# Gate and up matmuls, and the convolution's among them, as pairs of 64-row tiles ordered by GpSimd tokens

## The chip, the cores and the metric

The kernel runs on one core of one Trainium2 chip. A core has a matrix engine (TensorE, PE in the profile; its weight loads are PEld), a vector engine (VectorE, DVE), an activation engine (ScalarE, ACT), GpSimd (POOL) and SyncE (SP), which here issues nearly all DMAs. The engines run their own instruction queues in order and wait for one another by semaphores. The metric is the device time of one execution in microseconds (us). Engine times below are from one profiled execution.

## The reference

A block of a network with adaptive layer norm: a long gated convolution, then a gated MLP, both added to the input. Sequence length S is 2048, width D 576, hidden width F 4608, all in bfloat16.

```python
mod = (silu(c) @ w_mod).reshape(c.shape[0], 6, 1, -1)      # sa, ca, ga, sb, cb, gb
h = layernorm(x) * (1 + ca) + sa
x = x + ga * A(h, k, v, shift_k, ssm_k, ssm_D)
h = layernorm(x) * (1 + cb) + sb
x = x + gb * ((silu(h @ w1) * (h @ w3)) @ w2)

def A(q, k, v, shift_k, ssm_k, ssm_D):
    kv = causal_conv(k, shift_k, taps=4) * v
    y = irfft(rfft(pad(kv)) * rfft(pad(ssm_k)))[:S] + kv * ssm_D
    return q * y
```

## The kernel before

**The convolution.** The sequence is cut into 8 blocks of 256 rows. Each block is transformed with small cosine and sine bases held in `Fb` and `Fk` (functions `forward`, `forward2`: matmuls of 288 columns from L299 and L313, followed by a ScalarE copy). The spectra `X` and `V` are multiplied and summed on VectorE (`pair`, L405 to L412), and `inverse` (L539) transforms the sums back. `k_rows` (L364) turns the filter's rows with TensorE transposes into one PSUM tile, which ScalarE copies out. `turn` (L571) does the same with the normed rows, and `turned` (L601) writes them, scaled and shifted, into `h2T`, the MLP's input. Layer norm statistics come from ScalarE sums (`junk`, L440), and six small GpSimd instructions make the scales of them (`ln_scales`, L455 to L460).

**The MLP.** The 2048 rows are handled in four row blocks of 512. For each, `stream` makes the hidden rows `h3`, and `down` multiplies them by `w2` (L974). The 4608 hidden columns are 36 pieces of 128; an item of `stream` is one such piece for 512 rows (or two pieces for 256 rows). An item needs gate and up, each a sum over D = 576 = 4 x 128 + 64. `full` does the four full 128-row matmuls of gate and of up (L911). `rest` does the last 64 rows (L922): w1's last 64 rows lie in partitions 0 to 63 and w3's in 64 to 127 of the same weight slot, so the two run side by side in the two halves of the array. Then `hide` lets ScalarE apply silu to the gate (`sg`, L929), copy the up half (`u`, L931), and VectorE multiply them (`h`, L933).

Items are taken in groups of `size`: two everywhere, four in the last row block, where no convolution is left. For the first half of a group `full` comes first and `rest` after; for the second half `rest` comes first and `full` later, so the 64-row matmuls of a group stand together:

```python
for m in early:
    begin(m); full(m, True)
for m in early: rest(m, False)
for m in late:
    begin(m); rest(m, True)
for m in early: hide(m)
for m in late:
    full(m, False); hide(m)
```

**Mixing the two.** The convolution of the next blocks is written as generators that yield their estimated cost. After each item `advance` runs such steps until as much cost is spent as is due. So TensorE, ScalarE and VectorE each find convolution work between the items. The first stream works on 256 rows while block 1 is convolved (33 to 72 us). The second finishes the first row block (72 to 133 us): it goes back over the first 24 pieces for rows 256 to 511 and does the remaining 12 for all 512 rows, so that groups of weights for 256 and for 512 rows alternate. The next two streams (172 to 250 us, 292 to 370 us) and the last one (408 to 480 us) are whole. A scheduler of the language sets the final order of each engine's queue from the program's order and its own estimates.

**Buffers and queues.** Weights of four pieces (w1, w3 and their last rows) fill one of two `wst` buffers, loaded by four DMAs of SyncE's queue: two of 512 KB (L866) and two of 64 KB (L867). `w2` pieces use four `w2t` buffers (L967) on the same queue, as do the loads and stores of old spectra (`Xd`, `Vd`, L417 to L433) and of the inputs. PSUM is four tiles (`ps`) of two banks each, taken in turn by all matmul results: an item holds one tile, gate in one bank and up in the other; a convolution step holds one as well. `sg` and `u` have two buffers each.

## Time and profile before

The median of three runs is 519.97 us (519.77 to 522.16). The profiled execution spans 519.5 us from its first to its last instruction; the profile gives no other time of it.

| stage | from, us | to, us | length | TensorE busy | VectorE busy | ScalarE busy |
|---|---|---|---|---|---|---|
| first block | 0 | 33.0 | 33.0 | 25.4 | 28.3 | 21.1 |
| stream, 256 rows, with block 1 | 33.0 | 72.2 | 39.2 | 35.9 | 34.2 | 25.5 |
| rest of stream 0 | 72.2 | 133.1 | 60.9 | 56.0 | 57.3 | 47.4 |
| down 0 | 133.1 | 172.2 | 39.1 | 38.7 | 30.3 | 15.9 |
| stream 1 | 172.2 | 250.5 | 78.3 | 78.3 | 55.0 | 57.7 |
| down 1 | 250.5 | 292.1 | 41.6 | 39.5 | 40.9 | 16.6 |
| stream 2 | 292.1 | 370.4 | 78.3 | 78.3 | 58.8 | 53.7 |
| down 2 | 370.4 | 408.4 | 38.0 | 37.5 | 14.5 | 17.4 |
| stream 3 | 408.4 | 480.3 | 71.9 | 71.9 | 16.5 | 36.7 |
| down 3 and output | 480.3 | 519.5 | 39.2 | 35.4 | 5.5 | 1.1 |

Busy times are sums of the recorded instructions, with the ends of matmuls modelled, so that a full TensorE is not one at its peak. In the lines of the profile L911 is a line of the kernel; `ps<-h2T,wst` tells what is written from what; the number after x counts instructions; "idle before" is the engine's idle time just before such instructions, with what ended it. A line of the stages gives from:to, its length, busy time and count of PE, PEld, DVE, ACT and POOL, the granted TensorE clock, the DMA engines' share and GB/s. A line of the chain gives start, length and what ran.

### The profile page before, as it was taken

The numbers are of one execution on the slowest core, as the hardware profiler recorded it, in microseconds if no ns is written. First come the engines' busy times: TensorE is split into PE (matmuls) and PEld (weight loads), VectorE is DVE, ScalarE is ACT, GpSimd is POOL, SyncE is SP. The second block draws the span as 40 slices with busy tenths as digits, with TensorE's granted clock in tenths as the row PEclk, the third lists the DMA queues.
The fourth block names the chain that finished last, engine by engine and source line by source line (L and its number), as shares of the span: only waits on it lengthen the run. The fifth ranks groups of instructions, "written<-read, shape, count | busy, mean of one in ns | idle before, by whom it ended". The sixth has DMA issues, their size and how long they took to land.

```text
span 519.5 us, 8708 instructions
## 1 busy us (share of the span) xinstructions
PE 496.9 (96%) x3351; PEld 292.4 (56%) x3351; DVE 341.2 (66%) x515; ACT 293.0 (56%) x581; POOL 53.4 (10%) x109
## 2 busy tenths in 40 slices
PE   7889988998999999999998999999999999999997
PEld 3656765455787544444676643444578544444775
DVE  8887997999995355797999995389661212222012
ACT  6748669668553369759562465876815346445000
POOL 3403011203021001202002000120101000000000
PEclk9979999999999999999999999999999999999999
DMA  8948839757769953648999886454555553550462
GB/s 280 336 126 276 251 108 322 275 170 227 231 193 325 358 183 105 194 150 293 354 357 336 329 252 185 147 196 140 162 139 151 150 173 107 171 162 18 117 179 70
DMA packets 102205, 107.77 MB, mean 207 GB/s; under 512 B 5075, under 2 KB 94228, under 8 KB 102164
## 3 DMA queue, kind: packets, MB, share of 16 engines
q1 hardware_dynamic: 102142, 107.21, 65.5%
q8 instruction: 26, 0.43, 0.3%
q14 instruction: 15, 0.12, 0.1%
q10 hardware_dynamic: 22, 0.01, 0.0%
HBM read 96.00 MB, written 11.21 MB: 206 GB/s over the span
## 4 chain that ended last, share of the span: by engine, by line
PE 80%; DMA 10%; ACT 4%; DVE 3%; issue 1%; POOL 1%; SPq 1%; POOLq 0%; DVEq 0%; ACTq 0%
PE ps L911 44%; PE ps L974 23%; PE ps L922 7%; DMA wst<-in_B_w_dram 5%; DMA w2t<-in_B_w_dram 3%; PE ps L313 2%; PE ps L539 2%; DMA Xd<-X 1%; DMA knat<-in_A_ssm_k_dram 1%; PE ps L364 1%; PE ps L299 1%; ACT junk L440 1%; ACT sg L929 1%; PE ps L571 1%; ACT h2T L601 0%
## 5 line engine op out<-in xcount | busy, mean ns | idle before, releaser
L911 PE MATMUL ps<-h2T,wst 128*128 128x512 bf16 (+1 forms) x1344 | 268.0, 351 | 7.3 <-DMA wst<-in_B_w_dram 4.2
L911 PEld LDWEIGHTS <-wst 128*128 128x128 bf16 x1344 | 128.1, 98 | 130.3 <-issue 20.9
L929 ACT ACTIVATE sg<-ps 128x512 bf16<-128x512 f32 x144 | 86.9, 604 | 116.9 <-PE ps L922 74.2
L974 PE MATMUL ps<-w2t,h 128*128 128x288 bf16 x1152 | 145.4, 286 | 3.0 <-DMA w2t<-in_B_w_dram 2.4
L974 PEld LDWEIGHTS <-h 128*128 128x128 bf16 x1152 | 112.4, 98 | 32.3 <-issue 3.8
L933 DVE TENSOR_TENSOR h<-sg,u 128x512 bf16<-128x512 bf16 x144 | 60.3, 421 | 96.4 <-ACT u L931 96.4
L931 ACT CAST u<-ps 128x512 bf16<-128x512 f32 x144 | 84.7, 588 | 0.4 <-DVE h L933 0.4
L410 DVE TENSOR_TENSOR p<-X,V 128x3456 bf16<-128x3456 bf16 x28 | 54.6, 1952 | 5.8 <-DMA X<-Xd 5.1
L412 DVE TENSOR_TENSOR z<-z,p 128x3456 bf16<-128x3456 bf16 x28 | 54.6, 1951 | 0.2
L992 DVE TENSOR_TENSOR og<-ps,gbrow 128x288 bf16<-128x288 f32 x32 | 13.1, 449 | 48.9 <-PE ps L974 48.9
L922 PE MATMUL ps<-h2T,wst 64*128 64x512 bf16 (+1 forms) x336 | 42.9, 352 | 0.0
L440 ACT ACTIVATE junk<-x 128x576 bf16<-128x576 bf16 x54 | 37.6, 697 | 0.5
L601 ACT ACTIVATE h2T<-ps,sbcol,cbcol 128x256 bf16<-128x256 bf16 x35 | 16.7, 569 | 26.1 <-PE ps L571 26.1
L922 PEld LDWEIGHTS <-wst 64*128 64x128 bf16 x336 | 11.3, 94 | 27.5 <-issue 24.5
L455 POOL TENSOR_SCALAR l2m<-l2s 128x2 f32<-128x2 f32 x6 | 7.8, 1294 | 154.9 <-ACT junk L440 154.9
L334 DVE TENSOR_TENSOR kvt<-kh,shk 128x1152 bf16<-128x1152 bf16 x24 | 18.0, 752 | 6.8 <-DMA kh<-in_A_k_dram 6.7
L566 ACT ACTIVATE h2row<-x,l2n,l2r 128x576 bf16<-128x576 bf16 (+1 forms) x24 | 13.8, 653 | 11.4 <-POOL l2n L460 11.4
L455 POOL TENSOR_SCALAR l1m<-l1s 128x2 f32<-128x2 f32 x7 | 4.6, 662 | 141.2 <-ACT junk L440 141.2
L335 DVE TENSOR_TENSOR kv<-kv,kvt 128x1152 bf16<-128x1152 bf16 x24 | 18.1, 754 | 0.3
L315 ACT CAST X<-ps 128x576 bf16<-128x576 f32 x24 | 15.7, 666 | 0.0
L405 DVE TENSOR_TENSOR z<-X,V 128x3456 bf16<-128x3456 bf16 x7 | 13.7, 1951 | 1.4 <-DMA X<-Xd 1.4
L740 ACT CAST y<-ps 128x576 bf16<-128x576 f32 x14 | 8.4, 653 | 9.9 <-PE ps L539 9.8
(136 smaller groups left out, 353.3 us busy)
## 6 DMA issues: line engine op xcount, KB each, us to landing
wst<-in_B_w_dram SPq DMA_DIRECT2D x80, 512.0 KB, 4.7
w2t<-in_B_w_dram SPq DMA_DIRECT2D x72, 288.0 KB, 3.2
X<-Xd SPq DMA_DIRECT2D x8, 864.0 KB, 5.8
Xd<-X SPq DMA_DIRECT2D x6, 864.0 KB, 6.6
wst<-in_B_w_dram SPq DMA_DIRECT2D x80, 64.0 KB, 2.2
kh<-in_A_k_dram SPq DMA_DIRECT2D x7, 720.0 KB, 7.2
Vd<-V SPq DMA_DIRECT2D x4, 864.0 KB, 6.0
V<-Vd SPq DMA_DIRECT2D x4, 864.0 KB, 5.1
```

Of the source, the lines that this page charges most:

```text
L334: nc.vector.tensor_mul(tmp[:], kh[:, 3 - j:5 - j, :], tap(j))
L335: nc.vector.tensor_add(kv[:], kv[:], tmp[:])
L410: nc.vector.tensor_mul(p[:], X[:], V[:])
L412: nc.vector.tensor_add(z[:], z[:], p[:])
L440: self.nc.scalar.activation(junk[:], src[:, i, :], func, accum_out=out[:, col:col + 1])
L601: nc.scalar.activation(dst, src, ACT.Identity, bias=self.sbcol[:, ct:ct + 1], scale=self.cbcol[:, ct:ct + 1])
L911: nc.tensor.matmul(gus[k][:, i, a * n:(a + 1) * n], w[:, 5 * i + ct, (fi + a) * P:(fi + a + 1) * P], hT[:, ct, t0:t1], start=(first and ct ...
L922: nc.tensor.matmul(gus[k][:, i, a * n:(a + 1) * n], w[rows, 4, (fi + a) * P:(fi + a + 1) * P], hT[rows, 4, t0:t1], start=(first and a == 0 ...
L929: nc.scalar.activation(sg[:], gus[k][:, 0, :], ACT.Silu)
L931: nc.scalar.copy(u[:], gus[k][:, 1, :])
L933: nc.vector.tensor_mul(self.h3[:, f:f + m, t0:t1], sg[:].rearrange("p (a t) -> p a t", a=m), u[:].rearrange("p (a t) -> p a t", a=m))
L974: nc.tensor.matmul(acc[t], self.h3[:, f0 + f, t * P:(t + 1) * P], w[:, f, :], start=(f0 + f == 0), stop=(f0 + f == NF - 1))
```

## The change

Every gate and up matmul over 128 rows becomes two over 64 rows. An item is done in two parts. In the first, rows 0 to 63 feed the gate's bank while rows 64 to 127 feed the up bank, in side-by-side pairs for the four full pieces of D and the last 64 rows (five pairs). In the second the halves are swapped (four pairs): rows 0 to 63 feed the up bank, rows 64 to 127 the gate's. Since both halves of the rows then write each bank, one after the other, the second part must not begin before the first is done. A token sees to that: `token` issues a GpSimd memset of one element that waits for the first part's last matmul, and the second part's first matmul on the bank waits for this memset.

Between the two parts of an item, the stream issues the second part of the item before and the first part of the item after it, with a share of the convolution's steps after each part (5/9 and 4/9 of the former amount). The groups of two or four items and the parameter `size` are gone. While a stream runs, `halves` is set, and the convolution's matmuls (`forward`, `forward2`, `inverse`) go through `two_banks`, which does the same: first part, token, a pause that ends `advance`, and then the swapped part at the next `advance`. The transposes of `k_rows` and `turn` become pairs of 64-row transposes into two banks as well; `k_rows` then needs two ScalarE copies. Outside of the streams all stays 128 rows high.

```diff
--- before.py
+++ after.py
@@ -65,6 +65,44 @@
         self.xo, self.hg, self.accs, self.l1 = {}, {}, {}, {}
         self.X, self.V, self.Wl = {}, {}, {}
         self.n_w13, self.w13, self.kept = 0, {}, {}
+        self.halves = self.pause = False
+
+    def newest(self):
+        return self.nc.cur_bb.bb.instructions[-1]
+
+    def wait_for(self, later, first):
+
+        self.tc.add_manual_dep(
+            later, first.name,
+            mybir.DependencyInfo(mybir.DependencyClass.Sync, mybir.DependencyReason.DATA),
+            reason="both halves of the rows write this bank, one after the other")
+
+    def token(self):
+
+        first = self.newest()
+        self.nc.gpsimd.memset(self.tok[:], 0.0)
+        self.wait_for(self.newest(), first)
+        return self.newest()
+
+    def two_banks(self, outs, terms):
+
+        mm = self.nc.tensor.matmul
+        if not self.halves:
+            for n, term in enumerate(terms):
+                for i in range(2):
+                    mm(outs[i], *term(i, slice(0, P)), start=(n == 0), stop=(n == len(terms) - 1))
+            return
+        for swap in range(2):
+            for n, term in enumerate(terms):
+                for rows, i in ((slice(0, 64), swap), (slice(64, P), 1 - swap)):
+                    mm(outs[i], *term(i, rows), start=(swap == 0 and n == 0),
+                       stop=(swap == 1 and n == len(terms) - 1))
+                    if swap == 1 and n == 0 and i == 1:
+                        self.wait_for(self.newest(), mark)
+            if swap == 0:
+                mark = self.token()
+                self.pause = True
+                yield 0.0
 
     def ps(self, shape=(P, 2, 512), dtype=F32):
         return self.psum.tile(list(shape), dtype, name="ps", tag="ps")
@@ -74,6 +112,7 @@
         nc, const = self.nc, self.const
         nc.scalar.preload_act_table(ACT.Silu)
         self.ident = const.tile([P, P], BF16, name="ident")
+        self.tok = const.tile([1, 1], F32, name="tok")
         self.npi = const.tile([P, 1], F32, name="npi")
         self.ppi = const.tile([P, 1], F32, name="ppi")
         self.neghalf = const.tile([P, 2], F32, name="neghalf")
@@ -293,12 +332,10 @@
         nc = self.nc
         for e in range(2):
             for cs in range(2):
+                def term(cc):
+                    return lambda h, rows: (basis[rows, cc * (e + 1), cs], rhs[rows, cc, h * H:(h + 1) * H])
                 ps = self.ps()
-                for cc in range(2):
-                    for h in range(2):
-                        nc.tensor.matmul(ps[:, h, 0:H], basis[:, cc * (e + 1), cs],
-                                         rhs[:, cc, h * H:(h + 1) * H],
-                                         start=(cc == 0), stop=(cc == 1))
+                yield from self.two_banks([ps[:, h, 0:H] for h in range(2)], [term(cc) for cc in range(2)])
                 nc.scalar.copy(dst(e, cs).rearrange("p (h d) -> p h d", h=2), ps[:, :, 0:H])
                 yield 0.4
 
...
@@ -359,11 +396,22 @@
         nat = self.knat
         kT = self.kvp.tile([P, 2, D], BF16, name="kT", tag="kT")
         pt = self.ps((P, 2, 1024), BF16)
-        for cc in range(2):
-            for ct in range(5):
-                nc.tensor.transpose(pt[:, cc, ct * P:(ct + 1) * P], nat[:, ct, cc:B:2],
-                                    self.ident[:])
-        nc.scalar.copy(kT[:], pt[:, :, 0:D])
+        if self.halves:
+            for cc in range(2):
+                for ct in range(5):
+                    for half in range(2 if ct < 4 else 1):
+                        rows, at = slice(64 * half, 64 * half + 64), 320 * cc + 64 * ct
+                        nc.tensor.transpose(pt[:, half, at:at + 64], nat[rows, ct, cc:B:2],
+                                            self.ident[rows, rows])
+            for half, n in ((0, 5), (1, 4)):
+                nc.scalar.copy(_ap(kT, 64 * half, [[D, 2], [P, n], [1, 64]]),
+                               _ap(pt, 1024 * half, [[320, 2], [64, n], [1, 64]]))
+        else:
+            for cc in range(2):
+                for ct in range(5):
+                    nc.tensor.transpose(pt[:, cc, ct * P:(ct + 1) * P], nat[:, ct, cc:B:2],
+                                        self.ident[:])
+            nc.scalar.copy(kT[:], pt[:, :, 0:D])
         if 2 < s < NBLK - 1:
             self.load_k(s + 1)
         self.kT = kT
@@ -526,19 +574,16 @@
         nc.vector.tensor_sub(z[:, 1:3, :], z[:, 1:3, :], z[:, 4:6, :])
         return 3.0
 
-    def inverse(self, s, cc):
-        nc = self.nc
+    def inverse(self, s, cc, ps):
         z = self.accs[s]
-        ps = self.ps()
+
+        def term(b, cs, row):
+            return lambda h, rows: (self.Fb[rows, b, cs], z[rows, row, h * H:(h + 1) * H])
         if s < SPLIT:
             terms = [(3 * cc + (cc if e else 0), cs, 3 * e + cs) for cs in (1, 0) for e in range(2)]
         else:
             terms = [(3 * cc, 1, cc), (3 * cc, 0, 3 - cc)]
-        for i, (b, cs, row) in enumerate(terms):
-            for h in range(2):
-                nc.tensor.matmul(ps[:, h, 0:H], self.Fb[:, b, cs], z[:, row, h * H:(h + 1) * H],
-                                 start=(i == 0), stop=(i == len(terms) - 1))
-        return ps
+        yield from self.two_banks([ps[:, h, 0:H] for h in range(2)], [term(*t) for t in terms])
 
     def residual_row(self, s, cc, ps):
         nc = self.nc
@@ -568,8 +613,14 @@
 
     def turn(self, pt, cc):
         for ct in range(5):
-            self.nc.tensor.transpose(pt[:, cc, ct * P:(ct + 1) * P],
-                                     self.h2row[:, cc, ct * P:(ct + 1) * P], self.ident[:])
+            cols = slice(ct * P, (ct + 1) * P)
+            if not self.halves:
+                self.nc.tensor.transpose(pt[:, cc, cols], self.h2row[:, cc, cols], self.ident[:])
+                continue
+            for half in range(2):
+                rows, at = slice(64 * half, 64 * half + 64), 320 * cc + 64 * ct
+                self.nc.tensor.transpose(pt[:, half, at:at + 64], self.h2row[rows, cc, cols],
+                                         self.ident[rows, rows])
 
     def turn_split(self, cc):
 
...
@@ -876,8 +935,11 @@
                 break
             self.due -= c
             self.spent += c
-
-    def stream(self, r, jobs, rate, size):
+            if self.pause:
+                self.pause = False
+                break
+
+    def stream(self, r, jobs, rate):
 
 
 
...
@@ -902,26 +964,21 @@
             ws[job[0:3]] = w
 
 
-        def full(k, first):
+        def part(k, swap):
             (fc, t0, t1, _, _), fi, m = items[k]
             w, n = ws[fc, t0, t1], t1 - t0
             for a in range(m):
-                for i in range(2):
-                    for ct in range(4):
+                cols = slice((fi + a) * P, (fi + a + 1) * P)
+                for ct in range(4 if swap else 5):
+                    for rows, i in ((slice(0, 64), swap), (slice(64, P), 1 - swap)):
                         nc.tensor.matmul(gus[k][:, i, a * n:(a + 1) * n],
-                                         w[:, 5 * i + ct, (fi + a) * P:(fi + a + 1) * P], hT[:, ct, t0:t1],
-                                         start=(first and ct == 0 and a == 0),
-                                         stop=(not first and ct == 3 and a == m - 1))
-
-        def rest(k, first):
-            (fc, t0, t1, _, _), fi, m = items[k]
-            w, n = ws[fc, t0, t1], t1 - t0
-            for a in range(m):
-                for i in range(2):
-                    rows = slice(64 * i, 64 * i + 64)
-                    nc.tensor.matmul(gus[k][:, i, a * n:(a + 1) * n],
-                                     w[rows, 4, (fi + a) * P:(fi + a + 1) * P], hT[rows, 4, t0:t1],
-                                     start=(first and a == 0), stop=(not first and a == m - 1))
+                                         w[rows, 5 * i + ct if ct < 4 else 4, cols], hT[rows, ct, t0:t1],
+                                         start=swap == 0 and ct == 0 and a == 0,
+                                         stop=swap == 1 and ct == 3 and a == m - 1)
+                        if swap == 1 and ct == 0 and a == 0 and i == 1:
+                            self.wait_for(self.newest(), marks[k])
+            if swap == 0:
+                marks[k] = self.token()
 
         def hide(k):
             (fc, t0, t1, _, _), fi, m = items[k]
@@ -933,27 +990,22 @@
             nc.vector.tensor_mul(self.h3[:, f:f + m, t0:t1], sg[:].rearrange("p (a t) -> p a t", a=m),
                                  u[:].rearrange("p (a t) -> p a t", a=m))
             del gus[k]
-            self.advance(rate * 2.05)
 
         def begin(k):
             if items[k][1] == 0:
                 load(items[k][0])
             gus[k] = self.ps()
-        for k in range(0, len(items), size):
-            early, late = range(k, k + size // 2), range(k + size // 2, k + size)
-            for m in early:
-                begin(m)
-                full(m, True)
-            for m in early:
-                rest(m, False)
-            for m in late:
-                begin(m)
-                rest(m, True)
-            for m in early:
-                hide(m)
-            for m in late:
-                full(m, False)
-                hide(m)
+        self.halves = True
+        for k in range(len(items) + 1):
+            if k < len(items):
+                begin(k)
+                part(k, 0)
+                self.advance(rate * 2.05 * 5 / 9)
+            if k > 0:
+                part(k - 1, 1)
+                hide(k - 1)
+                self.advance(rate * 2.05 * 4 / 9)
+        self.halves = False
 
     def down(self, r, rate):
         nc = self.nc
@@ -1002,7 +1054,8 @@
         self.steps, self.due, self.spent = steps, due, 0.0
 
     def end(self):
-        self.advance(1e9)
+        while self.steps is not None:
+            self.advance(1e9)
 
     def run(self):
         self.setup()
...
```

## The prediction

> **What bounds the kernel now.** I read the page first, then the stages, then the chain of work that ended last, then what sits next to it: weight loads, PSUM evacuation, GpSimd.
>
> ```profile
> span 519.5 us, 8708 instructions
> PE 496.9 (96%) x3351; PEld 292.4 (56%) x3351; DVE 341.2 (66%) x515; ACT 293.0 (56%) x581; POOL 53.4 (10%) x109
> ...
> wst<-in_B_w_dram SPq DMA_DIRECT2D x80, 512.0 KB, 4.7
> ```
>
> TensorE is never idle for long. The stages (stretch, length, then busy time by engine) show where it is idle at all:
>
> ```profile
> 33.00:72.20 39.20, 35.88 (x310) 26.73 (x310) 34.20 (x56) 25.48 (x50) 6.09 (x8) 0.92 0.70 208
> 72.20:133.10 60.90, 55.98 (x412) 33.60 (x412) 57.30 (x75) 47.42 (x97) 10.75 (x18) 1.00 0.69 226
> 172.20:250.50 78.30, 78.30 (x405) 32.51 (x403) 54.97 (x82) 57.67 (x116) 7.72 (x18) 1.00 0.65 213
> 292.10:370.40 78.30, 78.30 (x405) 32.45 (x403) 58.83 (x83) 53.68 (x107) 4.86 (x12) 1.00 0.59 181
> 408.40:480.30 71.90, 71.90 (x363) 30.25 (x361) 16.54 (x42) 36.73 (x70) 0.00 (x0) 1.00 0.42 131
> ```
>
> These are the five gate/up streams: the first two (256-column items) have idle TensorE, the last three none. The chain in the fifth and in the second:
>
> ```profile
> 408.57 3.45 PE ps L911 x16
> 412.02 0.97 PE ps L922 x8
> 412.99 7.01 PE ps L911 x32
> ```
>
> ```profile
> 86.60 1.04 PE ps L911 x4
> ...
> 94.63 5.99 DMA wst<-in_B_w_dram
> 100.67 1.04 PE ps L911 x4
> ...
> 122.50 6.32 DMA wst<-in_B_w_dram
> 128.87 1.49 PE ps L911 x12
> ```
>
> Read from the first: a 512-wide matmul takes 3.45/16 = 0.2156 us. Eight 64-row ones are four side-by-side pairs, 0.8624 at that pitch; they take 0.97. The 32 full ones after them would take 6.90 and take 7.01. So each change of tile size costs 0.11, 0.22 there and back. Where four 64-row ones run (0.54 in the third and fourth stream), two pairs less are 0.43 less: a further pair costs 0.215, so pairs truly overlap. Read from the second: in the second stream the chain goes through weight loads, 6.0 to 6.3 us from issue to use.
>
> **What the change removes.** The excursions to 64 rows: 6 + 12 + 18 + 18 iterations of two items and 9 of four are 63, times 0.22 = 13.9 us. It keeps the changes at the stream ends, four in and four out, 0.9. An item stays nine slots (eight full and one pair before, nine pairs after). Net -13.0, if nothing else waits: -4.0 in the third and fourth stream each, -2.0 in the fifth, the rest in the first two.
>
> **Weights come free later.** There are two `wst` buffers. Before, the next load of a buffer goes out at its group's end and has the whole next group's time. After, the last part of a group is issued behind the first part of the next, and the first pair of any group needs both w1 (rows 0-63) and w3 (rows 64-127). Between a buffer's last and first read lie, behind a group of four items, three first parts and three second parts: 27 pairs x 0.2156 = 5.8 us (before 8.6); behind a 256-wide group of two items one of each, 1.9 us (before some 4.8). The load takes, by the chain, 6.0 to 6.9 from issue; 4.7 is the page's median, to which 0.6 comes for the second issue: 5.3 to 7.5 from release, and I take 6.2, as the second stream's rows show.
>
> - Second stream: groups of four and two alternate. The period of a pair of groups becomes 6.2 + 1.94 + 6.4 + 1.94 = 16.5: each buffer waits its load, then holds one first and one second part of the neighbour; 6.4 is 5.8 and the convolution's matmuls between. Now it is (128.87 - 100.67)/2 = 14.1. 2.4 x 3.5 pairs is +8.4; less 0.7, since the first group's wait is partly there already: +7.7. With 5.3 it is +5, with 7.5 (two loads late) +17.
> - First stream: two-item groups take 39.2/6 = 6.5 each; a loaded buffer would allow 6.2 + 1.94 = 8.1. Four groups wait for loads: +6.4, of which VectorE waits in the same stretch cover some; +4 (0 to 12).
> - Third and fourth: 5.8 to 6.9 against 5.3 to 6.2, so mostly in time; behind the loads of old spectra (864 KB) on the same queue it is late. +1 each (0 to 5).
> - Fifth: only these loads run; the first of each pair shows up after 3.8 to 4.1 there. 0.
>
> **PSUM.** Four double-bank tiles. An item lives over two parts of its own and two of its neighbours, and a convolution tile between them holds a third. I counted the matmul time between a tile's last matmul and the first of the tile four allocations later. Evacuation needs drain 0.16 (a matmul's 379 ns less its pitch), `sg`, `u`, and some 0.1 for the semaphores: 1.47.
>
> ```profile
> L929 ACT ACTIVATE sg<-ps 128x512 bf16<-128x512 f32 x144 | 86.9, 604 | 116.9 <-PE ps L922 74.2
> ...
> L931 ACT CAST u<-ps 128x512 bf16<-128x512 f32 x144 | 84.7, 588 | 0.4 <-DVE h L933 0.4
> ```
>
> In the third and fourth stream four items find 0.6 (0.87 short each) and six convolution tiles 1.2 (0.27 short): +5.1, bounds 2 (if part hides in other waits) and 8. In the first two streams such shortages, some 7 us, lie beside the load waits: nothing, and 7 if loads are in time.
>
> **Tokens.** Each first part is followed by a GpSimd memset that waits for TensorE; the first swapped weight load waits for it, and with it all of TensorE, then ScalarE's `sg`, VectorE's `h` and the release of `wst`. In most of the 196 cases 0.9 to 1.9 us of other matmuls lie between. The token: drain 0.16, memset 0.10, semaphores 0.2: 0.46, hidden. Eight convolution tokens have one pair between (0.11): 0.35 each, of which two lie in the third and fourth stream: +1 with the 0.7 tails (0 to 3). Ahead of the token stand the layernorm's six GpSimd instructions:
>
> ```profile
> 0.24 0.10 POOL L1084 MEMSET const-float32-0.0<- 128x1 f32 x1 [0.24 <-issue]
> ...
> 121.57 2.00 POOL L455 TENSOR_SCALAR l2m<-l2s 128x2 f32<-128x2 f32 x1 [25.82 <-ACT junk L440]
> 123.66 0.68 POOL L457 TENSOR_TENSOR l2r<-l2m 128x2 f32<-128x2 f32 x1
> ...
> 126.61 0.40 POOL L460 TENSOR_TENSOR l2n<-l2m,l2r 128x2 f32<-128x2 f32 x1
> ```
>
> That is 5.4 us here and 2.4 to 5.4 elsewhere. A token behind one of 3.3 us comes 0 to 1.8 late; six such sequences lie in the third and fourth stream: +4 (1 to 14, if `junk` too is late on ScalarE). Conversely the sequence waits for a token ahead of it, up to 2 us; `hg` and `h2row` wait for that, as they do now (11.4 us idle), off the path.
>
> The small instructions take 0.2 when undisturbed and up to 2.0 or 3.0 while VectorE works. If VectorE held a memset alike (its instructions last up to 1.95), convolution tokens with 0.9 to 1.1 would be late by up to 1.4: some 40 x 0.5 = +20, the upper end; the lower is 0.10 undisturbed, and I take that, the only memset rows. [...] No row shows a memset beside VectorE.
>
> **The rest.** 288-wide convolution matmuls become twice as many, in pairs: 0.1225 a pair if weight loads keep up (two 64-row loads of 94 ns start together at L922); 0. `k_rows` makes two ScalarE copies of one (1.13 us); ScalarE is 74% busy in the third stream; 0, at most 0.5 x 5. Extra yields only move convolution steps by a part.
>
> **The clock.**
>
> ```profile
> 30.00:31.00 1.00, 0.04 (x1) 0.04 (x2) 0.93 (x5) 0.48 (x1) 0.35 (x1) 1.00 0.86 294
> 33.00:34.00 1.00, 1.00 (x6) 0.30 (x5) 1.00 (x2) 0.61 (x2) 0.00 (x0) 0.50 0.00 0
> ```
>
> The granted clock (third from the end) fell to 0.50 from 32.4 to 39 us, after three microseconds (30 to 33) with TensorE mostly idle; the later waits, up to 2.0 us, left it at 1.00. Waits of 4 us for weights may bring it down again: 3.3 us lost each time, 0 to 4 times. I take 0, as half speed in a stream that waits for loads costs little. [...]
>
> **Sum.** Second stream +7.7, first +4; third and fourth -8.0 + 0.4 + 2 + 5.1 + 1 + 4 = +4.5; fifth -2.0: +14.2. 519.5 + 14.2 = 533.7; the median of the three runs, 519.97, stands 0.5 above the profiled span (which is all that the profile gives), so 534.
>
> **Rivals.**
> - *Faster.* Loads and tokens are all in time and only the mode changes go: -13.0 gives 507. It decides if a pair of 512 KB loads lands within 1.9 to 2.3 us of release in the second stream, or if something that waits for VectorE anyway fills the time. For it: 35.88 busy of 39.20 in the first stream, with VectorE 34.20. Against it: 5.99 and 6.32 above. Half of the load cost gives 515. 0.21.
> - *Held tokens.* VectorE holds the memsets: +20, 554. For it: 2.00 for L455; against it: most small rows at 0.2. 0.10.
> - *No net change.* The small ends of every bound: +5 + 0 - 8.0 + 0.4 + 2 + 1 - 2.0 = -1.6 to about +3; 518 to 522. 0.09.
> - *The change does nothing*, as pairs would not run side by side: 0.43 for two pairs excludes it.
>
> **How the numbers follow.** Forecast, 0.60: 534, its own range 522 to 550. 517.4 and 522.6 are 0.5%, about what a measurement of this kernel can tell from no change. Faster 0.21, same 0.08, slower 0.71. The range takes in most of the faster case and of the held tokens: 510 to 552.
>
> **What would show it.** Right: L922's pattern gone and item slots at 1.94; chain through `wst` in 33 to 145 us, with gaps of 2 to 4 us before each 256-wide group's neighbour; the fifth stream at 70 us; small waits of TensorE for GpSimd next to L455. Wrong: streams one and two no longer than 100 us; or memset rows of a microsecond; or waits on `sg` and `u` larger than on the weights.

## The result and the profile after

The changed kernel takes 601.27 us (median of four runs, 600.64 to 602.81) against 519.87 for the kernel before on the same chip: a ratio of 1.154, 95% interval 1.148 to 1.160. It is slower, as forecast, but by 81 us where 14 were forecast, and the time lies above the range. The profiled execution spans 599.5 us.

The page's head, the engines' busy time, the granted clock in 40 slices, and the weight loads (their number, size and median time to landing):

```profile
span 599.5 us, 12152 instructions
...
PE 513.7 (86%) x4881; PEld 325.0 (54%) x4881; DVE 345.9 (58%) x515; ACT 298.1 (50%) x586; POOL 65.6 (11%) x305
...
PEclk9887878898889999999979999998899999999999
...
wst<-in_B_w_dram SPq DMA_DIRECT2D x80, 512.0 KB, 4.1
```

TensorE was busy 96% of the span and is busy 86% now. VectorE and ScalarE do nearly the same work as before (341.2 and 293.0 us busy). The mean granted clock fell from 0.993 to 0.949. By stage (two stretches for stream 0, then streams 1, 2 and 3; columns as before):

```profile
32.70:90.00 57.30, 41.24 (x551) 32.06 (x552) 33.56 (x54) 23.91 (x47) 11.27 (x30) 0.79 0.49 149
90.00:178.70 88.70, 63.68 (x761) 41.49 (x757) 68.44 (x86) 50.55 (x103) 11.00 (x56) 0.90 0.46 153
218.20:313.70 95.50, 80.71 (x732) 42.33 (x732) 59.21 (x84) 58.96 (x116) 13.05 (x68) 0.95 0.53 180
357.90:452.30 94.40, 80.19 (x732) 40.61 (x731) 56.71 (x81) 57.33 (x114) 9.95 (x68) 0.96 0.45 143
489.80:560.30 70.50, 70.23 (x650) 31.40 (x650) 15.99 (x40) 37.29 (x70) 3.21 (x36) 1.00 0.42 133
```

Stream 0 grew from 100 to 146 us, streams 1 and 2 from 78 to 95 and 94, and stream 3 shrank from 71.9 to 70.5. The streams that run beside the convolution pay; the one without it gains. The chain in stream 0 (start, length, what ran) goes through loads as before:

```profile
44.43 1.91 PE ps L974 x16
...
47.33 5.89 DMA wst<-in_B_w_dram
53.23 0.05 issue
53.27 1.93 PE ps L974 x19
```

The load took 5.89, as long as before, and TensorE waits longer for such loads (19.7 us in all against 4.6, counted as below): they start too late, and don't last longer. The evacuation, to set beside the rows of it shown before, and the tokens (busy, mean ns of one, then idle before):

```profile
L986 ACT ACTIVATE sg<-ps 128x512 bf16<-128x512 f32 x144 | 86.2, 599 | 168.9 <-PE ps L974 131.0
...
L988 ACT CAST u<-ps 128x512 bf16<-128x512 f32 x144 | 83.9, 583 | 0.0
...
L83 POOL MEMSET tok<- 1x1 f32 x196 | 17.5, 89 | 366.0 <-PE ps L974 305.6
```

Neither step of the evacuation became dearer, and a token takes 89 ns (89 to 91 for all 196). What grew are the waits; from the list of waits (engine and line, who it waited for: us in all, times, longest):

```profile
ACT sg L986 <- DVE h L990: 37.6, 18, 3.8
...
PEld L974 <- DMA wst<-in_B_w_dram: 23.7, 13, 3.5
...
PEld L98 <- POOL tok L83: 16.6, 12, 4.3
...
PEld L974 <- POOL tok L83: 14.5, 4, 7.3
```

The first of them in the list of before:

```profile
ACT sg L929 <- DVE h L933: 7.1, 7, 1.7
```

TensorE's own waits from stream 0 on, taken from start to start of neighbouring matmuls wherever more than 0.5 us lies between, less the 0.216 of a pair, sum to 80.9 us against 11.7 before: 26.0 for tokens, 19.7 for `wst`, 24.6 for `u` (the release of a PSUM tile), and the rest for `w2t` and copies of the convolution. These sums are used below. The largest token wait, on GpSimd's row of time (start, length, instruction, idle before):

```profile
35.68 6.40 POOL L503 TENSOR_SCALAR l1m<-l1s 128x2 f32<-128x2 f32 x1 [1.11 <-ACT junk L488]
42.17 0.67 POOL L505 TENSOR_TENSOR l1r<-l1m 128x2 f32<-128x2 f32 x1
...
44.16 0.19 POOL L508 TENSOR_TENSOR l1n<-l1m,l1r 128x2 f32<-128x2 f32 x1
44.29 0.23 POOL L83 MEMSET tok<- 1x1 f32 x2
```

TensorE stood still from 37.4 to 44.4 for the two tokens of the last line. L503 waited for ScalarE's sums, then took 6.40 us (L504, of the same kind, took 0.19 at 42.81, just after VectorE had stopped) while eight VectorE instructions (0.42 to 1.95 us each) ran back to back. The typical wait for `u`, all engines in order of time:

```profile
275.70 1.95 DVE L460 TENSOR_TENSOR z<-z,p 128x3456 bf16<-128x3456 bf16 x1
275.70 0.58 ACT L988 CAST u<-ps 128x512 bf16<-128x512 f32 x1
276.33 2.12 PE L974 MATMUL ps<-h2T,wst 64*128 64x512 bf16 x18 [0.92 <-ACT u L988]
277.68 1.96 DVE L458 TENSOR_TENSOR p<-X,V 128x3456 bf16<-128x3456 bf16 x1
...
279.56 0.42 DVE L990 TENSOR_TENSOR h<-sg,u 128x512 bf16<-128x512 bf16 x1
...
280.07 0.60 ACT L986 ACTIVATE sg<-ps 128x512 bf16<-128x512 f32 x1 [3.79 <-DVE h L990]
280.57 0.58 ACT L988 CAST u<-ps 128x512 bf16<-128x512 f32 x1
281.20 1.04 PE L974 MATMUL ps<-h2T,wst 64*128 64x512 bf16 x8 [2.75 <-ACT u L988]
```

Read it backwards: TensorE waits for `u`; ScalarE could not empty that tile before `sg` had a free buffer; both buffers of `sg` were held until VectorE did `h`; and `h` stood behind two products of 1.95 us.

### The profile page after: what moved, and what is told of

Its sections match the earlier page's. It is cut to its first block, busy times and chain, and to the rows that moved or that the text cites. A ratio compares the mean times of both kernels' runs of the same rounds, so it can differ in the third digit from the quotient of the medians.

```text
span 599.5 us, 12152 instructions
## 1 busy us (share of the span) xinstructions
PE 513.7 (86%) x4881; PEld 325.0 (54%) x4881; DVE 345.9 (58%) x515; ACT 298.1 (50%) x586; POOL 65.6 (11%) x305
## 4 chain that ended last, share of the span: by engine, by line
PE 54%; DMA 13%; DVE 13%; ACT 11%; POOL 4%; issue 3%; SPq 1%; ACTq 0%; POOLq 0%
PE ps L974 29%; PE ps L1026 20%; DMA wst<-in_B_w_dram 7%; DMA w2t<-in_B_w_dram 4%; ACT junk L488 4%; DVE z L460 4%; DVE p L458 3%; ACT u L988 2%; ACT sg L986 2%; DMA h<-in_w_mod_dram 2%; POOL l1m L503 2%; PE ps L98 1%; PE ps L93 1%; ACT hg L548 1%; DVE h L990 1%
## 5 line engine op out<-in xcount | busy, mean ns | idle before, releaser
L974 PE MATMUL ps<-h2T,wst 64*128 64x512 bf16 (+1 forms) x3024 | 324.7, 364 | 46.9 <-DMA wst<-in_B_w_dram 19.0
L974 PEld LDWEIGHTS <-wst 64*128 64x128 bf16 x3024 | 170.4, 99 | 178.3 <-issue 30.3
L988 ACT CAST u<-ps 128x512 bf16<-128x512 f32 x144 | 83.9, 583 | 0.0
L83 POOL MEMSET tok<- 1x1 f32 x196 | 17.5, 89 | 366.0 <-PE ps L974 305.6
L488 ACT ACTIVATE junk<-x 128x576 bf16<-128x576 bf16 x54 | 37.1, 687 | 1.1
L98 PE MATMUL ps<-kv,Fb 64*128 64x288 bf16 x128 | 18.8, 306 | 14.4 <-POOL tok L83 7.9
L98 PEld LDWEIGHTS <-Fb 64*128 64x128 bf16 x208 | 14.2, 105 | 30.3 <-issue 13.3
L453 DVE TENSOR_TENSOR z<-X,V 128x3456 bf16<-128x3456 bf16 x7 | 13.7, 1956 | 9.8 <-PE ps L93 4.2
L611 ACT ACTIVATE h2row<-x,l2n,l2r 128x576 bf16<-128x576 bf16 (+1 forms) x24 | 13.7, 647 | 6.8 <-POOL l2n L508 6.8
L98 PE MATMUL ps<-kT,Fk 64*128 64x288 bf16 x64 | 10.1, 296 | 5.7 <-POOL tok L83 4.3
```

Of the source, the lines that this page charges most:

```text
L83: self.nc.gpsimd.memset(self.tok[:], 0.0)
L98: mm(outs[i], *term(i, rows), start=(swap == 0 and n == 0), stop=(swap == 1 and n == len(terms) - 1))
L488: self.nc.scalar.activation(junk[:], src[:, i, :], func, accum_out=out[:, col:col + 1])
L974: nc.tensor.matmul(gus[k][:, i, a * n:(a + 1) * n], w[rows, 5 * i + ct if ct < 4 else 4, cols], hT[rows, ct, t0:t1], start=swap == 0 and c ...
L988: nc.scalar.copy(u[:], gus[k][:, 1, :])
```

## The experiments

Four theories. A: tokens queue behind the layernorm's scales on GpSimd. B: weights come late. C: tiles come free late, in two forms: C1, because ScalarE is held (by VectorE's `h`, or by its own earlier work); C2, because four tiles are too few for items in two parts, whoever empties them. D: waits bring the clock down and so cost more than themselves. Each run is given with its ratio to the kernel before on the same chip (519.9 to 522.1 us). Stage lengths are of single profiled executions, from the first matmul of a stage to the first of the next.

**The scales and the weights, one by one and together.**

```diff
-        e.tensor_single_scalar(mean[:], ssum[:], -1.0 / D, op=ALU.mult)
...
-        e.tensor_mul(nmr[:], mean[:], rstd[:])
+        e.memset(rstd[:], 20.0)
+        e.memset(nmr[:], 0.0)
```

> The changed kernel (601.3 us), but the layernorm's six GpSimd instructions (L503 to L508) become two memsets of constants that wait for nothing; this leaves the computing of mean and deviation out, and all else stays. In the changed kernel's trace eight waits of TensorE for a token, 27 us together (the longest 7.3), end just behind such a sequence. Theory A (tokens queue behind the layernorm's scales, in order on GpSimd, and these wait for ScalarE's sums and beside VectorE): these eight waits go and some lost clock with them; time 601 - 27 - 5 = 569, between 560 and 578, and what is left of TensorE's waits for GpSimd is under 3 us. Rival C (these waits only stand in for others: PSUM tiles, weights, the layernorm's own chain): the waits move to u, sg and wst, and the time stays at 588 to 601.

583.4 us, ratio 1.124 (1.120 to 1.127). TensorE's waits for tokens fell from 26.0 to 1.2, as A says, but those for `u` rose from 24.6 to 28.0 and for `wst` from 19.7 to 23.8. The layernorm's scales are a cause worth 18 us, not 32: part of these waits stood in for others. The edit also frees ScalarE, whose `h2row` and `hg` had waited for these scales (6.8 and 1.7 us in the changed kernel's list); no run takes this part from the tokens' part.

```diff
     def load_w13(self, fc):
...
         self.w13[fc] = t
+        if self.n_w13 > NW13:
+            return
```

> The changed kernel, but the gate and up weights are loaded for the first two groups only; every later group reads what lies in the two buffers, so the loads are left out and the matmuls are the same. Theory B (weights late): the waits of TensorE for wst in the first stream, 19.8 us of the trace, go, with some clock: 601 - 20 - 5 = 576, between 568 and 582. Rival C (the waits move to PSUM and tokens): 590 to 601.

591.6 us, 1.139 (1.134 to 1.143). The waits for `wst` are gone, and those for `u` rose to 37.1. B alone is worth 10 us; about half of the 19.7 moved. Stream 0 became 14.9 shorter, and the down stage behind it 5.2 longer.

> Both edits together: constants for the layernorm's scales, and weights loaded for the first two groups only. If A and B are causes that add up: 601 - 27 - 20 - 10 = 544 (535 to 555), and what TensorE still waits for is u, sg and kT, some 29 us. If waits only move, 575 or more. If PSUM's shortage was itself caused by the other two (bunched items behind each long wait), it goes as well: 515 to 530.

572.1 us, 1.102 (1.098 to 1.106): 29.2 less, about the sum of the two (17.9 and 9.6). The expected 544 did not come: with both away the waits for `u` are 41.8, and 52 us remain over the kernel before. The largest cause was still in place.

> The control: the kernel before the change with the same two edits, constants for the layernorm's scales and weights loaded for the first two groups only. It had 4.6 us of waits for weights and none for GpSimd: 520 - 5 = 515 (512 to 518). If these edits took 29 us from the changed kernel for a reason that has nothing to do with the change, it falls much further, to 500 or below.

521.1 against 521.2, 1.000 (0.998 to 1.002), where 515 was expected. The control stays where it was: the 29 us belong to the change.

**What holds the tiles.** Both kernels start from the one with 572.1 us.

```diff
-            sg = self.hp.tile([P, RB], BF16, name="sg", tag="sg")
-            nc.scalar.activation(sg[:], gus[k][:, 0, :], ACT.Silu)
+            f = fc * FC + fi
+            sg = self.h3[:, f:f + m, t0:t1]
+            nc.scalar.activation(sg, gus[k][:, 0, :].rearrange("p (a t) -> p a t", a=m), ACT.Silu)
...
+            nc.vector.tensor_mul(sg, sg, sg)
```

> The kernel with constants for the scales and two weight loads (572.1 us), and now ScalarE's silu goes straight to its own place in h3 and VectorE squares it there, so sg and its two buffers are gone and ScalarE never waits for VectorE's h (the product with u is left out; every engine keeps as many instructions of the same size). In that kernel's trace TensorE still waits 42 us for u (31 waits), and ScalarE's sg waits 52.7 us for h (22 times). Theory C1 (VectorE, in order and busy with the convolution's products, holds sg, ScalarE then holds PSUM): the waits for u fall to 10 us or less, time 572 - 32 - 6 of clock = 534 (525 to 545). Theory C2 (four PSUM tiles are too few for tiles that live over two parts, whoever empties them): waits for u stay above 30, time 562 to 572.

544.3 us, 1.045 (1.041 to 1.049). The edit takes away ScalarE's wait for VectorE's `h` (for the buffers of `sg`, and for those of `u`, which VectorE no longer reads) and gives 27.8 us; waits for `u` fell from 41.8 to 17.0, with the same four PSUM tiles. Streams 1 and 2 fell from 91.4 and 89.7 to 84.1 and 81.9. That is C1, the largest single cause.

```diff
-        self.halves = True
         for k in range(len(items) + 1):
...
-        self.halves = False
```

> The kernel with constants for the scales and two weight loads (572.1 us), but the convolution's matmuls inside the streams keep 128 rows, as before the change: their PSUM tiles live over one step and no token is issued for them; gate and up stay in staggered pairs. C2, by the convolution's tiles: waits for u fall from 42 to 20 or less; against that stands a change of tile size for each of some 80 steps, 0.22 each, +13 (to +17): 572 - 22 - 5 + 13 = 558 (550 to 566). C1: waits for u stay at 35 or more, and the time rises by the size changes, 575 to 585.

570.1 us, 1.095 (1.091 to 1.098): 2 us less, waits for `u` 35.4. The convolution's longer-lived tiles are not the main cause. The time fits neither theory: what the shorter tiles gave and what the changes of tile size cost cannot be told apart here. The longer lives of the gate and up tiles are not tested by it.

The longest wait left in `lnr_free_sg` (ScalarE in order of time; TensorE waited from 252.6 to 256.3 for `u`):

```profile
250.73 1.63 ACT L544 ACTIVATE hg<-x,l1n,l1r 128x576 bf16<-128x576 bf16 x2
252.26 0.68 ACT L488 ACTIVATE junk<-x 128x576 bf16<-128x576 bf16 x1
...
254.55 0.58 ACT L985 ACTIVATE h<-ps 128x512 bf16<-128x512 f32 x1
255.02 0.67 ACT L488 ACTIVATE junk<-x 128x576 bf16<-128x576 bf16 x1
...
255.69 0.57 ACT L987 CAST u<-ps 128x512 bf16<-128x512 f32 x1
```

Here ScalarE's own order holds the tile: layernorm work first, the evacuation after. So these sums were taken away as well:

```diff
     def ln_sums(self, src, i, ssum, ssq, col=None):
...
+        return
```

> The kernel without the scales' computing, without weight reloads and without the sg buffers (544.3 us), and now also without the layernorm's sums on ScalarE (L488, junk: 54 activations of 0.67 us with their readings are left out). In its trace the longest waits left in the streams end behind such sums: 3.5 us at 256.3, where four of them and two hg stood ahead of the evacuation on ScalarE. Theory: what is left of the waits for u (17 us) is ScalarE's own order; they fall to 8 or less, the third and fourth stream go from 84.1 and 81.9 to about 78, and the time to 544 - 11 - 5 of clock = 528 (522 to 534). Rival (four PSUM tiles are too few whatever stands before them on ScalarE): waits for u stay at 14 or more and the time at 538 or more.

530.6 us, 1.019 (1.015 to 1.023). Waits for `u` are 6.2, and streams 1 and 2 take 77.5 and 78.8, as expected. The sums are worth 13.7 us. With ScalarE prompt, four tiles are nearly enough for items in two parts: C2 alone does not make the waits.

> The control for all four edits: the kernel before the change with constants for the scales, two weight loads, silu straight into h3 and no layernorm sums. If before's order of full and 64-row matmuls had slack for all of these, the edits are worth nothing to it beyond its few waits: 521 - 2 to 6 = 517 (514 to 521), and TensorE's stream lengths stay at 78.3, 78.3 and 71.9. If it gains 20 us or more, the edits are no test of the change.

514.2 us, 0.987 (0.983 to 0.991): all four edits give the kernel before 8 us, nearly all in stream 0, and the changed kernel 70.7. The streams step by step (us):

| kernel | stream 0 | 1 | 2 | 3 | time |
|---|---|---|---|---|---|
| before | 100.2 | 78.2 | 78.3 | 71.8 | 519.9 |
| changed | 146.1 | 95.5 | 94.4 | 70.5 | 601.3 |
| scales constant | 134.1 | 92.5 | 90.7 | 71.1 | 583.4 |
| and no weight reloads | 119.9 | 91.4 | 89.7 | 70.0 | 572.1 |
| and `sg` not held | 111.6 | 84.1 | 81.9 | 70.0 | 544.3 |
| and no sums | 105.9 | 77.5 | 78.8 | 70.0 | 530.6 |
| before, all four edits | 93.4 | 78.2 | 78.3 | 71.9 | 514.2 |

With the four edits the two kernels differ by 16 us where they differed by 81: these causes account for 65. The 16 lie mostly in stream 0 (12.5); there the longest wait left is 5.8 us for a token, behind a constant's memset that itself waits for ScalarE's `hg`.

**The same edge alone, and a remedy that leaves nothing out.**

> The changed kernel with that one edit alone: silu goes straight to its own place in h3 and VectorE squares it there (the product with u is left out), scales and weight loads as in the changed kernel. It took 28 us where scales and weights were out of the way. If the causes add up: 601 - 28 = 573 (566 to 580). If ScalarE's wait is hidden behind the waits for tokens and weights: 585 to 598.

588.7 us, 1.130 (1.125 to 1.135): alone the edit gives 12.6, where it gave 27.8 with tokens and weights in time. Waits for tokens (25.7) and `wst` (22.0) remain and hide the rest. The causes do not add up in any order.

```diff
-NW2 = 4
+NW2 = 3
...
-        self.hp = pool("hp", bufs=2)
+        self.hp = pool("hp", bufs=3)
```

> A remedy that leaves nothing out: the changed kernel (601.3 us) with three buffers for sg and u in place of two, and three for the second weights (w2t) in place of four to make room. C1 says that ScalarE's waits for VectorE's h (37.6 us) hold PSUM; with one buffer more half or more of them are bridged: 601 - 15 - 3 = 583 (575 to 592), down stages 0 to 2 us longer each. If two buffers are not what holds ScalarE: 598 to 605.

618.4 us, 1.188 (1.183 to 1.194), slower than the changed kernel. ScalarE's waits for `h` fell from 37.6 to 18.5 as expected; but with one `w2t` buffer less TensorE's waits for `w2t` rose from 4.9 to 14.3, and on the same queue those for `wst` from 19.7 to 26.1. The room that the third buffer took was worth more where it was.

**Why before did not suffer.** Theory R: in the kernel before, PSUM tiles in reserve hide the holds. Its rival H: such holds cost whatever the tiles' lives.

```diff
-            u = self.hp.tile([P, RB], BF16, name="u", tag="u")
+            u = self.hp.tile([P, RB], BF16, name="u", tag="sg")
```

> The kernel before the change, with u taken from the two buffers of sg, so that each sg has to wait for the product h of the item just before (in effect one buffer each in place of two); everything is computed. ScalarE's waits for h (7.1 us before, 37.6 in the changed kernel) should grow to 40 us or more. Theory R (a reserve of PSUM tiles hides them, since a tile of before is written in about one item's time and not over two parts): TensorE's waits for u stay under 8 us and the time at 521 to 527. Rival H (such holds cost whatever the tiles' lives, and before merely had fewer of them): waits for u of 20 us or more, 540 or more.

536.0 us, 1.030 (1.025 to 1.035). Its list of waits:

```profile
ACT sg L929 <- DVE h L933: 75.3, 84, 3.7
```

That is twice the hold of the changed kernel (37.6). Streams 1 and 2 became 80.5 and 79.8, about 2 us longer; TensorE's waits for `u` came to 13.9, half of it one wait of 7 us at 138, in stream 0. The time lies between the two theories; in streams 1 and 2 the kernel before swallowed most.

```diff
-        self.psum = pool("psum", bufs=4, space=bass.MemoryType.PSUM)
+        self.psum = pool("psum", bufs=3, space=bass.MemoryType.PSUM)
...
-            tail = r == NRB - 1 and h == 1
+            tail = False
```

> The kernel before the change with three double-bank PSUM tiles in place of four (and the last stage without its own split of the tail, which three tiles do not allow); everything is computed. Theory R: with about one tile of reserve gone, as the staggered parts take it, TensorE waits for u and the clock falls: streams of 78.3 become 85 to 95, the first two together 100 become 108 or more, the time 545 to 580. Rival H: the tiles are not what hides ScalarE's holds, 521 to 530.

540.6 us, 1.039 (1.034 to 1.044). Streams 1, 2 and 3 take 81.4, 83.9 and 76.2: a tile less costs 3 to 6 us each, less than R expected.

> The kernel before the change with both of the last two edits: u from sg's buffers, and three PSUM tiles in place of four. If the two only add: 521 + 15 + 19 = 555, the third and fourth stream 78.3 + 2.3 + 3.2 = 84 and 78.3 + 1.5 + 5.6 = 85. If they multiply, as theory R says (a hold costs once no tile is in reserve): these streams 90 or more, as after the change (95), waits of TensorE for u 40 us or more, time 570 or more.

553.7 us, 1.061 (1.053 to 1.069), streams 1 and 2 at 84.1 and 88.2: they add up and do not multiply. R as stated falls: the lost reserve is a cost, but together with the holds it makes 6 and 10 us of these streams, not 16.

```diff
+        while self.due > 0 and self.steps is not None and not (self.halves and self.long):
...
+            self.long = self.long or c > 1.9
...
                 hide(k - 1)
+                self.long = False
```

> The changed kernel, but a step of the convolution that puts a 2-us product on VectorE ends the steps until the next item's h is recorded; nothing is left out. In VectorE's order two such products stand between two h's 4, 2 and 4 times in the first three parts with convolution (3, 1 and 0 before the change); with this edit 5, 3 and 1 times. If this placement is what makes ScalarE wait (the third such part, 94.4 us, against 78.3 before): that part falls by 6 us or more, the other two stay, time 592 or less. If not: 94 stays within 3 us, time 598 to 605.

601.4 us, 1.151 (1.142 to 1.161): no change in the time. Streams 1 and 2 fell by 3 each, whether two products stood together more or less often, and the following down stages grew by 2 and 4.5. The placement of the products is not it either. What stays open is how the 16 us of such a stream divide between tiles that live long and the dependence of each second part on token, tile and weights at once; no run here takes the stagger away alone.

**The pairs by themselves, and the clock.** In `last_only` the old order of items stays for streams 0 to 2, and stream 3 alone runs in pairs.

```diff
-            self.stream(r, jobs, rate)
+            self.stream(r, jobs, rate, 4 if r == NRB - 1 else 2, r in PAIRS)
...
+PAIRS = (3,)
```

> The staggered pairs in the last stream alone (fifth stretch, where no convolution and no layernorm runs beside it); the other streams are those of the kernel before. My prediction's term for it: 9 excursions of 0.22 us less = -2.0; the changed kernel's trace shows 70.5 against 71.9 us for that stream, -1.4. So 519.9 - 1.4 to 2.0 = 518.2 (517.8 to 518.6). Rival (pairs themselves are slower or cost a clock dip): 520 or more. Should it come out as expected it is a version faster than both kernels.

520.22 against 520.10 us, ratio 1.0004 (0.9985 to 1.0022): no change that can be measured, where 518.2 was expected. The stream took 71.0 in the profiled execution, with one wait of 1.1 for `wst` in it (start to start); in the five profiles of pairs whose stream 3 loads no weights it took 70.0, 1.8 less than before. So the saving is there, and one late load eats half of it.

```diff
+        self.ntok = getattr(self, "ntok", -1) + 1
+        for d in range({6: 3, 13: 4, 20: 5, 27: 6}.get(self.ntok, 0)):
+            self.nc.gpsimd.memset(self.h2row[:], 0.0)
+            self.wait_for(self.newest(), first)
+            first = self.newest()
```

> The clock by itself, in the quiet last stream: the kernel that has pairs in the last stream alone (520.2 us, profiled span 517.9), with 3, 4, 5 and 6 extra GpSimd memsets of 128x1280 (estimated 1.2 us each) ahead of four of its tokens, seven items apart, so that TensorE waits an estimated 2.1, 3.3, 4.5 and 5.7 us there. Theory D (a wait of some 3 us or more brings the granted clock to 0.50 for several us, as in the first 6 us of work in the trace of before): the clock falls to 0.50 behind the second, third and fourth wait, not the first, and each costs about 3.3 us more than itself: 517.9 + 15.6 + 10 = 543. Rival (the clock answers to something else, mean load or power): it stays at 1.00 behind all of them, 517.9 + 15.6 = 533.

536.2 us (one round; 1.028, 1.025 to 1.031). TensorE's four waits (idle time in brackets), and the 5 us behind each (the clock is third from the end):

```profile
422.77 14.22 PE L1001 MATMUL ps<-h2T,wst 64*128 64x512 bf16 x130 [2.01 <-POOL tok L89]
439.73 10.32 PE L1001 MATMUL ps<-h2T,wst 64*128 64x512 bf16 x94 [2.74 <-POOL tok L89]
458.45 13.52 PE L1001 MATMUL ps<-h2T,wst 64*128 64x512 bf16 x107 [3.32 <-POOL tok L89]
478.65 3.68 PE L1001 MATMUL ps<-h2T,wst 64*128 64x512 bf16 x20 [3.23 <-POOL tok L89]
```

```profile
422.80:427.80 5.00, 5.00 (x48) 2.27 (x50) 0.85 (x2) 2.21 (x5) 0.23 (x3) 1.00 0.15 36
439.80:444.80 5.00, 5.00 (x48) 2.27 (x50) 0.85 (x2) 2.66 (x6) 0.20 (x3) 1.00 0.09 26
458.45:463.45 5.00, 5.00 (x32) 2.00 (x34) 0.76 (x2) 2.15 (x4) 0.18 (x2) 0.66 0.00 0
478.70:483.70 5.00, 5.00 (x32) 1.98 (x34) 0.85 (x2) 2.15 (x4) 0.22 (x3) 0.66 0.55 164
```

After 2.0 and 2.7 us of idleness the clock stays, after 3.3 and 3.2 it is 0.66 on average over 5 us: 16 matmuls fewer in the same time, 1.7 us lost each. So a wait does cost more than itself here, as D says, at half of the price expected; the waits themselves came out shorter than estimated. That their length decides is not shown: in the changed kernel a wait of 2.75 us was followed by a lower clock as well (0.68 over 3.3 us, in the last section).

## Why the prediction was wrong

The direction was right. The forecast's own sum, term by term:

- **Mode changes, -13.0.** Right where nothing waits: -2.0 was said for stream 3, and it is 1.8 shorter when its weights are there. In stream 1 of the table's row "and no sums" (77.5 us, clock 1.00) five waits of 0.5 to 1.2 us from start to start are left, 2.8 in all beyond a pair's pitch; 77.5 - 2.8 is 3.5 below the 78.2 of before, near the -4.0 of the sum.
- **Weights late, +13.7** (7.7 and 4 in stream 0, 1 each in streams 1 and 2). Taking the loads away gave 9.6 alone and 11.3 beside constant scales: the right size. Of the terms that add time it was the only large one that the sum had right.
- **Layernorm ahead of tokens, +4.** It measured 17.9. In streams 1 and 2 it was 3.0 and 3.7, inside the bounds 1 to 14; in stream 0, where the sum had put nothing, it was 12.0. The sum let one such instruction take "up to 2.0 or 3.0" us and all six 2.4 to 5.4; the first one in stream 0 took 6.40 by itself.
- **PSUM, +5.1.** The step that failed. "Evacuation needs drain 0.16 (a matmul's 379 ns less its pitch), `sg`, `u`, and some 0.1 for the semaphores: 1.47" is the evacuation by a ScalarE that is free (its own terms give 1.45). The list of waits before already had `sg` waiting for `h` (7.1 us in 7 waits, up to 1.7); it was left out of the sum, and so were the layernorm's sums on ScalarE. Both together measured 27.8 + 13.7 = 41.5 us with the other two causes away. In streams 1 and 2, for which the sum had 5.1 (2 to 8), they gave 13.9 and 10.9. For stream 0 it took nothing, "and 7 if loads are in time"; there, with loads in time, the two gave 14.0.
- **Clock, 0 (bounds 0 to 13).** The changed kernel's 4881 matmuls are busy 513.7 us; the same 4881 with the four causes away, 491.0. The difference, 22.7 us, is the same work done more slowly, most of it at a lower clock (0.949 in the mean against 0.983). The waits of these two differ by 80.9 - 30.5 = 50.4; 50.4 + 22.7 make 73, and the spans differ by 70.7. So a us of wait cost some 0.4 us more on average. That "half speed in a stream that waits for loads costs little" did not hold.
- **Held tokens (rival, 554).** As stated it falls: all 196 memsets take 89 to 91 ns, also beside VectorE (0.09 at 432.10, during its product of 1.96 us from 430.34). The hold came one instruction ahead of the token: L503 took 6.40 us beside VectorE. That VectorE held L503 is the author's reading of these rows; no run shows it by itself, and L504, of the same kind, took 0.19 at 337.92 with VectorE busy too.
- **Faster, no net change.** Neither. Their condition, tokens and loads in time, held in stream 3 alone; and where two edits brought it about, the kernel still took 572.1.

The prediction's last paragraph named a sign of being wrong that came: "waits on `sg` and `u` larger than on the weights" (TensorE's 24.6 for `u` against 19.7 for `wst`, behind ScalarE's 37.6 for `h`). Its other two, streams one and two no longer than 100 us and memset rows of a microsecond, did not come.

## What to carry to other kernels

Before an order is staggered, count the evacuation with everything that its engine does in order, the buffers it writes to and the readers of these: a chain TensorE, ScalarE, VectorE is as late as what is queued in front of its last member, here two products of 1.95 us. A semaphore that is carried by an otherwise idle engine is only as prompt as what that engine runs ahead of it, waits included: here an instruction of 6.40 us ahead of two tokens of 89 ns. Price waits of TensorE at more than themselves: in `gaps` each of two falls of the clock cost 1.7 us more, and between the changed kernel and the one with the four causes away a us of wait cost some 0.4 us more on average.

## What was not expected of the hardware

- In these traces the length of a single wait does not tell by itself which clock follows. In the quiet stream 2.74 us idle left it at 1.00 and 3.23 was followed by 0.66 over 5 us, as shown. In the changed kernel 2.75 us idle at 281.2, with another 0.92 idle five us earlier, was followed by a mean of 0.68 over 3.3 us.
- In the changed kernel the granted clock was at 0.50 in 14 stretches of 3.4 to 10.2 us, 61.4 us in all, and at 1.00 in the rest of the span. From 279.0 to 282.4, where it fell, TensorE was busy for 1.20 us. The first fall, at 26.4, comes during 60 matmuls of one column, and from 23.0 to 26.4 the profile counts TensorE as busy all the time. No run moves one wait while all else stays, so what decides whether the clock falls is not shown.
- A GpSimd TENSOR_SCALAR of 128x2 took 0.19 or 6.40 us within ten us of time, the latter while VectorE ran without a pause, as shown.
- Pairs of 64-row matmuls 512 wide keep up a pitch of 0.216 us over a whole stream (69.7 us for 324 pairs in stream 3 with its weights there), where a 128-row matmul of the kernel before took 0.2156: half the rows at a time, issued in pairs, cost TensorE nothing here.
